# Two attention-and-mixer layers on one core: cutting the second layer's keys where the mixers finish, and more places for filler matmuls

## The chip, the cores and the metric

The kernel runs on one core of one Trainium2 chip. The metric is device time in microseconds (us) of one execution. All engines of the core work from instruction lists that are fixed at build time: TensorE (PE) multiplies matrices, ScalarE (ACT) does exponentials and GELUs, VectorE (DVE) and GpSimd (POOL) do element-wise work, and SyncE (SP) issues most transfers (DMAs).

## The reference

The input x is 2048 rows of 448 numbers. Two equal layers with shared weights follow each other; each is an attention part A and a mixer part B, both on a normalised x and both added back:

```
x = x + A(layernorm(x))      # 16 heads of 28: softmax(q k^T / sqrt(28)) v, then @ wo
x = x + B(layernorm(x))
# B(x): h  = gelu(layernorm(x) @ w1); its four column groups are shifted by +1, -1, +2, -2 rows
#       x1 = x + shifted(h) @ w2
#       return x1 + gelu(layernorm(x1) @ w3) @ w4
```

Because the mixer shifts rows by at most two, a tile of 128 rows can be mixed as soon as its two neighbours have left the attention. The second layer's attention needs the keys of all rows for each query row.

## The kernel before, in words

**Tiles and segments.** The 2048 rows are 16 tiles of 128. Keys, queries and values are made by projections from a transposed, normalised copy of x (xT), which is loaded from DRAM (xnd) into one of two buffers (XT, L654). The 16 heads are four groups g of four heads. CHUNKS (L493) cuts the queries into chunks of 4 tiles (the last one of the second layer into 2 and 2). ORDER (L494) lists, for each layer, which query chunk meets which range of key tiles: an entry (query chunk, first key tile, end key tile) becomes four segments, one for each g. In the second layer it begins

```
(0, 0, 4), (0, 4, 8), (1, 0, 8), (0, 8, 12), (1, 8, 12), (0, 12, 16), (1, 12, 16), (2, 0, 16), ...
```

so the first two query chunks take the keys in parts, as these become ready. Keys are projected in chunks of 4 tiles.

**The stream.** A block is one head, one key tile and 512 queries. All blocks of both layers stand in one list. They are grouped into 819 units of alternately 3 and 2 blocks. Unit by unit PE writes scores into banks 0 to 2 or 3 and 4 of PSUM (`score_ops`, L1125, recorded at L1138), ACT takes the exponential of the unit in one instruction (`t_exp`, L1213), and PE multiplies it with the values into bank 5 (`t_pv`, recorded with other plain matmuls at L697). The units alternate between the two sets of banks. The other projections, mixer products and statistics share the banks that `misc` (L678) gives: banks 6 and 7, and, before the stream holds them, also 5, 4 and 3.

**The running bound.** Instead of a row maximum, the exponent is shifted by a bound from the norms of queries and keys. `k_proj` (L960) projects the keys of a chunk for one g, squares them and reduces the squares to a maximum (kmaxc, L981); `t_bias` (L1086) turns the maxima of all chunks so far into the bound; `q_proj` (L986) adds it to the queries. If a later part of the keys brings a larger bound, `t_fct` (L1104) makes the difference (dbc, L1108) and a factor for what is accumulated, and `t_qp` (L1155) corrects the queries (L1160). So a part of the keys can only begin when all chunks that it reaches have their maxima, for all four g.

**The mixers.** When all four g of a query chunk have been normalised (`t_norm`, L1319: sums to DRAM and back, otn at L1357), `t_outproj` (L1393) makes the output projection (added to x_res at L1408), `t_mixA` (L1429) the first half of the mixer, and `t_mixB` (L1566) the second half. Since a tile needs its right neighbour, the second half runs in groups of tiles 0-2, 3-6, 7-10, 11-13 and 14-15 in the first layer (BGROUPS, L1419). GELUs stand on ACT between the exponentials, with a table load before and after. Then `t_ln1_l1` (L926) normalises a finished tile and stores it for the second layer.

**What sets the order.** A planner (`Sched`, L175) runs at build time. It holds a generator for each piece of work with a priority (smaller goes first), a cost for each instruction (`c_ps` for DVE reading PSUM, `c_act`, `c_mm`, fixed numbers for small operations), and writes each engine's list in the order of its own clock. MIXP (L442) gives the priorities of mixers, KVP (L446) those of key, value and query projections of a chunk: in the second layer 3 for chunk 0 and 1.5 for the others; the mixers of the first layer's last chunk have 1.6.

**Filler.** `keep_pe_busy` (L268) puts filler matmuls (L1643, four matmuls of 256 columns each) into gaps of PE's plan, when the share of work in the last WIN us is below TARGET. A filler writes only into bank 6 or 7 and only while nothing holds that bank.

**The beginning.** `t_ln1_first` (L877) normalises and transposes the first four tiles, projects g = 0 and lets the stream start; g = 1 to 3 follow. For g = 0 the squares are taken by ACT straight from PSUM (`square_first`, L954) and the query's own norm is added in PSUM; for the others POOL squares the copy in SBUF (`square`, L957) and DVE adds the norm (L1027).

Of the kernel before, what the change touches and what calls it, by code (L numbers as in the profile page):

```python
# [174 lines left out]
class Sched:  # L175
    LAT = 0.2
    EARLY = 0.25
    WIN = 3.42
    TARGET = 0.5

    def __init__(self, P):
        self.P = P
        self.cur = {e: 0.0 for e in ENGS}
        self.tasks = []
        self.seq = 0
        self.pe_mode = None
# [9 lines left out]
        self.recent = []  # L196

# [4 lines left out]
    def _advance(self, t):  # L202
        changed = False
        while True:
# [13 lines left out]
            elif c == "sig":  # L218
                self.events.add(spec[1])
                self.evt_t[spec[1]] = self.clock  # L220
            elif c == "rel":
                self.busy[spec[1]] = False
# [45 lines left out]
    def keep_pe_busy(self, until):  # L268
# [3 lines left out]
        while self.cur["pe"] + dur + 0.12 < until:  # L272
# [7 lines left out]
            for b in banks:  # L280
                if self.busy.get(b, False):
# [14 lines left out]
    def run(self):  # L296
        P = self.P
        while True:
# [121 lines left out]
            op = P.add(eng, fn, reads, writes, kw.get("deps", ()), dma, t_end)  # L420
            if start > self.clock:
# [20 lines left out]
def MIXP(L, ch):  # L442
    return {(0, 0): 3, (0, 1): 3, (0, 2): 1.6, (0, 3): 1.6, (1, 0): 3, (1, 1): 3, (1, 2): 2.5, (1, 3): 2, (1, 4): 1.6}[(L, ch)]


def KVP(L, c):  # L446
    return {(0, 1): 1.5, (0, 2): 1.6, (0, 3): 1.7, (1, 0): 3, (1, 1): 1.5, (1, 2): 1.5, (1, 3): 1.5}[(L, c)]
# [6 lines left out]
def build_kernel(nc, A_x, A_wqkv, A_wo, B_x, B_w1, B_w2, B_w3, B_w4, out, n_layers=2):  # L454
# [23 lines left out]
    def c_ps(n):  # L478
        return 0.07 + n * 0.00104
# [10 lines left out]
    def c_mm(n):  # L490
# [4 lines left out]
             1: [(0, 0, 4), (0, 4, 8), (1, 0, 8), (0, 8, 12), (1, 8, 12), (0, 12, 16), (1, 12, 16), (2, 0, 16), (3, 0, 16), (4, 0, 16)]}  # L495

    segs = []
    for L_ in range(2):
        for (ch_, a_, b_) in ORDER[L_]:
            for g_ in range(4):  # L500
                segs.append((L_, ch_, g_, (a_ // 4, b_ // 4), list(range(a_, b_)), a_ == 0, b_ == NT))
    first_e = {}
    for L_ in range(2):
        for (ch_, a_, b_) in ORDER[L_]:
            if a_ == 0:
                first_e[(L_, ch_)] = b_ // 4
# [75 lines left out]
    with st:  # L582
# [40 lines left out]
        kmaxc = sb("kmaxc", [128, 2, 4, NCH], FP32)  # L623
        k2 = sb("k2", [128, 2, 5, 4], FP32)
        bcb = sb("bcb", [128, 2, 5, 4], BF16)
        bc29 = sb("bc29", [128, 2, 5, 4], FP32)
        dbc = sb("dbc", [128, 2, 5, 4], FP32)
        db29 = sb("db29", [128, 2, 5, 4], FP32)
        fct = sb("fct", [128, 2, 5, 4], FP32)
# [48 lines left out]
        def misc(*reads):  # L678
            return ("acq", MISC if ("tail",) in SC.events else MISC[0:5], list(reads))
# [7 lines left out]
        def kslot(L, c):  # L687
            return c if L % 2 == 0 else (4, 5, 0, 1)[c]

        def vslot(L, t):  # L690
            return 4 * kslot(L, t // 4) + t % 4
# [60 lines left out]
        def t_setup():  # L752
# [39 lines left out]
            b = yield ("acq", MISC[0:5])  # L792
# [41 lines left out]
        def stats(src, t, rkeys):  # L834
            yield op("dve", 0.55, lambda e: e.bn_stats(out=st6[:, t, :], in_=src), reads=rkeys, writes=[("st6", t)])
            yield op("dve", 0.12, lambda e: e.bn_aggr(out=mv[:, t, :], in_=st6[:, t, :]), reads=[("st6", t)], writes=[("mv", t)])
# [103 lines left out]
        def load_xT(L, c, xt):  # L940
            for t in range(4 * c, 4 * c + 4):
                yield ("wait", ("xnd", L, t))
            yield dma("sp", lambda e: e.dma_start_transpose(out=xT[:, xt, :, :], in_=xnd[512 * c:512 * c + 512, :]),
                      reads=[("xnd", t) for t in range(4 * c, 4 * c + 4)], writes=[(("xT", xt), i) for i in range(4)], t=TRL_T)


        def proj(xt, g, wpad, wnm):
            b = yield misc(("xT", xt), (wnm,))
            for fc in FCS:
                yield op("pe", c_mm(512), mm4(ps[:, bi(b), :], wpad[:, fc, 128 * g:128 * g + 128], xT[:, xt, fc, :], fc == 0, fc == 3),  # L950
# [3 lines left out]
        def square_first(b, si):  # L954
            return op("act", c_act(512), lambda e: e.activation(out=sq[:, si, :], in_=ps[:, bi(b), :], func=ACT.Square), reads=[("ps", bi(b))], writes=[("sq", si)])

        def square(si, src, rk):  # L957
            return op("pool", 1.2, lambda e: e.tensor_tensor(out=sq[:, si, :], in0=src, in1=src, op=ALU.mult), reads=rk, writes=[("sq", si)])  # L958

        def k_proj(L, c, g, xt):  # L960
            b = yield from proj(xt, g, wk_pad, "wk_pad")
            c0 = kcol(L, 4 * c)
            dst = kT[:, g, c0:c0 + 512]
            dk = [("kT", g, vslot(L, 4 * c + i)) for i in range(4)]
            fast = L == 0 and c == 0 and g == 0
            if fast:
                s = yield ("acq", SQ)
                si = num(s)
                yield square_first(b, si)
            yield op("dve", c_ps(512), lambda e: e.tensor_scalar(out=dst, in0=ps[:, bi(b), :], scalar1=MK, scalar2=None, op0=ALU.add),  # L970
                     reads=[("ps", bi(b)), (("cols",), 2)], writes=dk, touch=[b],
                     alt=[alt("act", c_act(512), lambda e: e.activation(out=dst, in_=ps[:, bi(b), :], func=ACT.Identity, bias=MK))])
            yield ("rel", b)
            if not fast:
                s = yield ("acq", SQ, dk)
                si = num(s)
                yield square(si, dst, dk)
            b2 = yield misc(("sq", si))
            yield op("pe", c_mm(512), mm4(ps[:, bi(b2), :], astat[:, :], sq[:, si, :], True, True), reads=[("sq", si), ("astat",)], writes=[("ps", bi(b2))], touch=[b2], mode="col4")
            yield ("rel", s)  # L980
            yield op("dve", c_ps(512), lambda e: e.reduce_max(out=kmaxc[:, L, g, c:c + 1], in_=ps[:, bi(b2), :], axis=AX.X),  # L981
# [4 lines left out]
        def q_proj(L, qc, g, xt):  # L986
# [6 lines left out]
            p0 = first_e[(L, [ci for ci in range(len(CHUNKS[L])) if CHUNKS[L][ci][0] // 4 == qc][0])]  # L993
# [746 lines left out]
```

## Time and profile before

| | us |
|---|---|
| median of 3 runs | 1208.27 |
| lowest and highest run | 1207.6, 1210.52 |
| profiled execution, its own time | 1204.26 |
| span in its trace | 1202.5 |
| PE busy in the span | 1058.9 |
| ACT busy in the span | 1059.7 |
| DVE busy | 452.2 |
| POOL busy | 382.7 |

The trace comes from one profiled execution. Its own time is the span from the first to the last instruction and 1.76 us around it; it lies 4.01 us under the median of the plain runs. In a row of a timeline the first number is the start in us from the beginning of the span, the second the time taken (of a run of equal instructions from the start of the first to the end of the last), then engine, line, operation, what is written and read, and in brackets the idle time of that engine just before it with what ended it. A row of a group gives the count, the busy time in us and the mean of one instruction in ns.

### The profile page before, as it was taken

What the parts mean: (1) busy time and instruction counts of PE and PEld (TensorE: products, weight loads), DVE (VectorE), ACT (ScalarE), POOL (GpSimd) and SP (SyncE); (2) the same over time, 40 slices, a digit from 0 to 9 for tenths busy, and PEclk for the clock granted to TensorE, in tenths of its full rate; (3) what the DMA queues carried; (4) which work ended last, traced back from release to release, by engine and by line L of the source; (5) the groups of instructions that cost most, each with busy time, mean ns of one, the idle gap of its engine ahead of it and who ended that gap; (6) DMA issues with size and microseconds to landing.
All of it is one profiled execution on the core that took longest, in us unless ns stands there. A gap on an engine that the chain in (4) does not pass through costs nothing.

```text
span 1202.5 us, 34008 instructions
## 1 busy us (share of the span) xinstructions
PE 1058.9 (88%) x15542; PEld 417.7 (35%) x15542; DVE 452.2 (38%) x921; ACT 1059.7 (88%) x906; POOL 382.7 (32%) x396
## 2 busy tenths in 40 slices
PE   5998888889888899898988998988889898889888
PEld 2333333343323332223332433332323433334355
DVE  8464213331242235331643353423352433233243
ACT  3768999999989999989999958998989999899932
POOL 4931114403325054412343240202427501252201
PEclk9899999899979999998998999998999998899899
DMA  3384112002111032011231021324321110220000
GB/s 102 83 242 103 38 51 46 15 17 71 27 30 29 11 107 46 11 19 48 75 94 35 20 90 44 106 89 112 60 38 35 26 45 22 45 47 11 10 17 22
DMA packets 95784, 64.28 MB, mean 53 GB/s; under 512 B 64664, under 2 KB 84440, under 8 KB 95640
## 3 DMA queue, kind: packets, MB, share of 16 engines
q1 hardware_dynamic: 92376, 57.63, 19.2%
q0 software_dynamic: 2304, 3.67, 1.2%
q8 instruction: 122, 2.00, 0.7%
q10 hardware_dynamic: 960, 0.80, 0.2%
q14 instruction: 22, 0.18, 0.1%
HBM read 28.16 MB, written 16.76 MB: 37 GB/s over the span
## 4 chain that ended last, share of the span: by engine, by line
ACT 40%; PE 37%; DMA 8%; DVE 7%; POOL 5%; issue 1%; SPq 0%; ACTq 0%; POOLq 0%; DVEq 0%
ACT PT L1213 34%; PE ps L706 21%; PE ps L1138 9%; PE ps L697 6%; DMA rb<-rscr 4%; ACT h2T L1604 3%; POOL xn L850 2%; DMA xT<-xnd 1%; POOL otn L1357 1%; ACT hT L1488 1%; DMA rscr<-rT 1%; PE ps L1643 1%; DVE kmaxc L981 1%; DMA rT<-ub 1%; ACT L1604 1%
## 5 line engine op out<-in xcount | busy, mean ns | idle before, releaser
L1213 ACT ACTIVATE PT<-ps 128x1536 bf16<-128x1536 f32 (+1 forms) x819 | 939.3, 1307 | 59.2 <-PE ps L1138 56.6
L1138 PE MATMUL ps<-qT,kT 32*128 32x512 bf16 (+1 forms) x2304 | 326.5, 368 | 52.2 <-ACT PT L1213 43.6
L697 PE MATMUL ps<-PT,vaug 128*32 128x512 bf16 (+1 forms) x2304 | 254.1, 367 | 2.0 <-DVE ub L1335 2.0
L1138 PEld LDWEIGHTS ps<-qT,kT 32*128 32x128 bf16 x2304 | 80.3, 91 | 342.6 <-ACT PT L1213 271.7
L1643 PE MATMUL ps<-wq_pad,ident 128*32 128x256 bf16 x3836 | 182.4, 282 | 2.1 <-DVE x1b L1547 1.0
L706 PE MATMUL ps<-xT,w 128*32 128x512 bf16 (+1 forms) x2240 | 173.2, 367 | 6.9 <-issue 4.7
L706 PE MATMUL ps<-w,h2T 128*32 128x448 bf16 x1792 | 123.5, 382 | 20.8 <-ACT h2T L1604 20.8
L1357 POOL TENSOR_TENSOR otn<-ub,rb 128x512 bf16<-128x512 f32 (+1 forms) x32 | 38.6, 1205 | 320.6 <-DMA rb<-rscr 314.1
L1643 PEld LDWEIGHTS ps<-wq_pad,ident 128*32 128x32 bf16 x3836 | 108.9, 98 | 43.3 <-issue 23.8
L1594 DVE CAST h2T<-ps 128x512 bf16<-128x512 f32 (+2 forms) x126 | 73.9, 586 | 121.0 <-PE ps L706 112.6
L697 PEld LDWEIGHTS ps<-PT,vaug 128*32 128x32 bf16 x2304 | 69.8, 95 | 102.1 <-issue 85.4
L706 PEld LDWEIGHTS ps<-xT,w 128*32 128x32 bf16 x2240 | 59.0, 96 | 63.8 <-issue 38.1
L706 PEld LDWEIGHTS ps<-w,h2T 128*32 128x32 bf16 x1792 | 49.7, 102 | 68.6 <-issue 27.3
L850 POOL TENSOR_SCALAR xn<-x_res,mv,mst 128x448 bf16<-128x448 f32 x30 | 55.6, 1865 | 1.9 <-DVE mst L1451 1.9
L958 POOL TENSOR_TENSOR sq<-qT 128x512 bf16<-128x512 bf16 x31 | 32.1, 1040 | 73.0 <-DVE qT L1001 68.8
L850 POOL TENSOR_SCALAR xn<-x1b,mv,mst 128x448 bf16<-128x448 f32 x29 | 54.5, 1879 | 1.7 <-POOL mst L1553 0.2
L1333 DVE COPY ub<-ps 128x512 f32<-128x512 f32 (+1 forms) x36 | 22.7, 630 | 85.4 <-PE ps L697 85.2
L958 POOL TENSOR_TENSOR sq<-kT 128x512 bf16<-128x512 bf16 x31 | 32.2, 1041 | 66.6 <-DVE kT L970 63.5
L706 PE MATMUL ps<-w,hT 112*32 112x448 bf16 x512 | 40.9, 414 | 13.8 <-ACT hT L1488 13.5
L706 PE MATMUL ps<-xT,wq_pad 128*32 128x512 bf16 x512 | 44.8, 420 | 6.2 <-DMA xT<-xnd 5.5
L706 PE MATMUL ps<-wo_pad,otn 128*32 128x448 bf16 x512 | 42.0, 378 | 9.1 <-POOL otn L1357 6.1
L1604 ACT ACTIVATE h2T<-h2T 128x7168 bf16<-128x7168 bf16 (+2 forms) x9 | 45.1, 5015 | 3.9 <-DVE h2T L1594 3.8
(134 smaller groups left out, 869.4 us busy)
## 6 DMA issues: line engine op xcount, KB each, us to landing
uscr<-ub SPq DMA_DIRECT2D x28, 256.0 KB
ub<-uscr SPq DMA_DIRECT2D x28, 256.0 KB
rb<-rscr SPq DMA_DIRECT2D x28, 256.0 KB
xnd<-xn SPq DMA_DIRECT2D x28, 128.0 KB, 2.0
x_res<-in_A_x_dram POOLq DMA_DIRECT2D x16, 224.0 KB, 3.5
xd<-x_res SPq DMA_DIRECT2D x16, 224.0 KB, 2.1
x_res<-xd SPq DMA_DIRECT2D x16, 224.0 KB
out_dram<-obf SPq DMA_DIRECT2D x16, 112.0 KB
```

The source lines that it names most:

```text
L697: return lambda e: e.matmul(out=out, lhsT=lhsT, rhs=rhs, start=start, stop=stop, **kw)
L706: r.append(e.matmul(out=out[c:c + w, :], lhsT=lhsT[:, c:c + w], rhs=rhs, start=start, stop=stop, tile_position=(0, c)))
L850: yield op(eng, dur, lambda e: e.tensor_scalar(out=xn[:, k, 0:D], in0=src, scalar1=scalar1, scalar2=scalar2, op0=ALU.subtract, op1=ALU.mul ...
L958: return op("pool", 1.2, lambda e: e.tensor_tensor(out=sq[:, si, :], in0=src, in1=src, op=ALU.mult), reads=rk, writes=[("sq", si)])
L981: yield op("dve", c_ps(512), lambda e: e.reduce_max(out=kmaxc[:, L, g, c:c + 1], in_=ps[:, bi(b2), :], axis=AX.X), reads=[("ps", bi(b2))], ...
L1138: yield op("pe", max(0.055, 0.22 / nc_ * NW / 512.0), lambda e, i=i, kc=kc, j=j, g=g, a=a, NW=NW, bank=bank: e.matmul(out=ps[:, bank, i * ...
L1213: yield op("act", 0.07 + n * 0.427, lambda e, bk=bk, s0=s0, n=n: e.activation(out=PT[:, s0:s0 + n, :], in_=ps[:, bk[0]:bk[0] + n, :], func ...
L1333: yield op("dve", c_ps(NW), lambda e: e.tensor_copy(out=u, in_=ps[:, 5, 0:NW]), reads=[("ps", 5)], writes=[uk])
L1357: yield op("pool", 0.2 + NW * 0.0021, lambda e: e.tensor_tensor(out=otn[:, g, 0:NW], in0=u, in1=rb[:, 0:NW], op=ALU.mult), reads=[uk, ("rb ...
L1594: ev = op("dve", c_ps(NW), lambda e, fch=fch, b=b: e.tensor_copy(out=h2T[:, fch, 0:NW], in_=ps[:, bi(b), 0:NW]), reads=[("ps", bi(b))], wr ...
L1604: yield op("act", c_act(14 * NW), lambda e: e.activation(out=h2T[:, :, 0:NW], in_=h2T[:, :, 0:NW], func=ACT.Gelu_apprx_tanh), reads=allk, ...
L1643: return [e.matmul(out=ps[32 * c:32 * c + 32, bi(b), 0:256], lhsT=ident[:, 32 * c:32 * c + 32], rhs=wq_pad[:, 0, 0:256], start=True, stop= ...
```

## The change

1. The second layer's keys are projected in chunks of 3, 4, 4, 3 and 2 tiles (a new table KC) in place of four chunks of 4. Bounds, maxima and transposed loads follow the new chunks (there are five for the second layer), with narrower projections for 3 and 2 tiles; the keys and values of the second layer lie in other places of their buffers.
2. The second layer's first two query chunks take the keys in parts of 7, 4 and 5 tiles, one after the other.
3. Priorities: the mixers of the first layer's last chunk go from 1.6 to 1.4, the second layer's key chunks 1 and 2 from 1.5 to 2.5; chunk 4 gets 1.5.
4. In the first layer's first chunk all four g take the short way: squares by ACT, the query's norm added in PSUM.
5. `misc` gives banks 6, 7 and 5 in place of 6, 7, 5, 4 and 3 (also in the set-up). `q_proj` waits for its bound before it takes a bank, except for the very first.
6. Filler: WIN 2.3 for 3.42, TARGET 0.52 for 0.5, and seven banks (6, 7, 0 to 4) for two. A bank may be filled while it is "dead", that is from the planned end of its last reader (the exponential, or the release of the bank) until PE writes it again.
7. The planner's costs for several DVE and POOL instructions are other numbers, mostly larger for DVE; the instructions are the same.

The core of the diff:

```diff
-    WIN = 3.42
-    TARGET = 0.5
+    WIN = 2.3
+    TARGET = 0.52
...
-                if self.busy.get(b, False):
+                if b not in self.dead:
...
-(0, 3): 1.6, (1, 0): 3, ...
+(0, 3): 1.4, (1, 0): 3, ...
...
-    return {..., (1, 0): 3, (1, 1): 1.5, (1, 2): 1.5, (1, 3): 1.5}[(L, c)]
+    return {..., (1, 0): 3, (1, 1): 2.5, (1, 2): 2.5, (1, 3): 1.5, (1, 4): 1.5}[(L, c)]
...
-        return 0.07 + n * 0.00104
+        return 0.13 + n * 0.00108
...
-             1: [(0, 0, 4), (0, 4, 8), (1, 0, 8), (0, 8, 12), (1, 8, 12), (0, 12, 16), (1, 12, 16), (2, 0, 16), (3, 0, 16), (4, 0, 16)]}
+             1: [(0, 0, 7), (1, 0, 7), (0, 7, 11), (1, 7, 11), (0, 11, 16), (1, 11, 16), (2, 0, 16), (3, 0, 16), (4, 0, 16)]}
+    KC = {0: [(0, 4), (4, 4), (8, 4), (12, 4)], 1: [(0, 3), (3, 4), (7, 4), (11, 3), (14, 2)]}
+
+    def kc_of(L, t):
+        return [c for c, (a, n) in enumerate(KC[L]) if a <= t < a + n][0]
+
+    def ext_of(L, t):
+        return 0 if t == 0 else kc_of(L, t - 1) + 1
...
-            return ("acq", MISC if ("tail",) in SC.events else MISC[0:5], list(reads))
+            return ("acq", MISC if ("tail",) in SC.events else MISC[0:3], list(reads))
...
-            return 4 * kslot(L, t // 4) + t % 4
+            return t if L == 0 else (t + 17 if t < 7 else t - 7)
...
-            fast = L == 0 and c == 0 and g == 0
+            fast = L == 0 and c == 0
...
+            if idx > 0 or g > 0:
+                yield ("wait", ("bc", L, p0, g))
             b = yield from proj(xt, g, wq_pad, "wq_pad")
...
-            if idx == 0 and g == 0:
+            if idx == 0:
...
+                for b in bk:
+                    yield ("dead", "b%d" % b)
                 yield ("sig", ("ex", u))
...
-        SC.fill = (0.12, filler, ["b6", "b7"], lambda b: ("ps", bi(b)), [("ident",), ("wq_pad",)])
+        SC.fill = (0.12, filler, ["b6", "b7", "b0", "b1", "b2", "b3", "b4"], lambda b: ("ps", bi(b)), [("ident",), ("wq_pad",)])
```

More of the change, by code (lines that the diff above doesn't have):

```diff
@@ L196, in __init__ @@
         self.recent = []
+        self.dead = set("b%d" % i for i in range(8))
+        self.bank_of = {("ps", i): "b%d" % i for i in range(8)}
     def spawn(self, gen, prio=5):
@@ L960, in k_proj, with square @@
+        def square(si, src, rk, NW=512):
+            return op("pool", 0.15 + NW * 0.0018, lambda e: e.tensor_tensor(out=sq[:, si, 0:NW], in0=src, in1=src, op=ALU.mult), reads=rk, writes=[("sq", si)])
         def k_proj(L, c, g, xt):
[L961 to L964, printed above, removed]
-            fast = L == 0 and c == 0 and g == 0
+            t0, n = KC[L][c]
+            NW = 128 * n
+            b = yield from proj(xt, g, wk_pad, "wk_pad", NW)
+            c0 = kcol(L, t0)
+            dst = kT[:, g, c0:c0 + NW]
+            dk = [("kT", g, vslot(L, t0 + i)) for i in range(n)]
+            fast = L == 0 and c == 0
@@ L1032, in v_proj @@
             yield ("wait", ("vinit",))
-            for i in range(4):
-                t = 4 * c + i
+            t0, n = KC[L][c]
+            for i in range(n):
+                t = t0 + i
                 vs = vslot(L, t)
@@ L1047, in t_kv @@
         def t_kv(L, c):
-            for t in range(4 * c, 4 * c + 4):
+            t0, n = KC[L][c]
+            for t in range(t0, t0 + n):
                 yield ("wait", ("xnd", L, t))
@@ L1077, in t_q @@
             xt = num(x_)
-            yield from load_xT(L, qc, xt)
+            yield from load_xT(L, 4 * qc, 4, xt)
             yield ("sig", ("qloaded", L, qc))
```

104 lines of the change are left out of this document (54 added, 50 removed).

## The prediction

> **What bounds the kernel now.** I read the page first, then ACT's timeline around each gap, then what PE and DVE do there.
>
> ```profile
> PE 1058.9 (88%) x15542; PEld 417.7 (35%) x15542; DVE 452.2 (38%) x921; ACT 1059.7 (88%) x906; POOL 382.7 (32%) x396
> ACT  3768999999989999989999958998989999899932
> L958 POOL TENSOR_TENSOR sq<-kT 128x512 bf16<-128x512 bf16 x31 | 32.2, 1041 | 66.6 <-DVE kT L970 63.5 <-PE ps L706 3.1
> L1213 ACT ACTIVATE PT<-ps 128x1536 bf16<-128x1536 f32 (+1 forms) x819 | 939.3, 1307 | 59.2 <-PE ps L1138 56.6
> L1643 PE MATMUL ps<-wq_pad,ident 128*32 128x256 bf16 x3836 | 182.4, 282 | 2.1 <-DVE x1b L1547 1.0
> ```
>
> The slices of ACT are the reading: 9 nearly everywhere, low in the first three, 5 once in the middle, low in the last two. In between the stream of exponentials is the bound: 819 units in 939.3 us, 1.147 us each. PE's 88% holds 182.4 us of filler, so it has room. A change gains only where ACT has no unit to work on. The start:
>
> ```profile
> 23.59 1.45 ACT L1213 ACTIVATE PT<-ps 128x1536 bf16<-128x1536 f32 x1 [1.22 <-PE ps L1138]
> 35.97 3.28 ACT L1213 ACTIVATE PT<-ps 128x1024 bf16<-128x1024 f32 x3 [10.92 <-PE ps L1138]
> 42.95 21.92 ACT L1213 ACTIVATE PT<-ps 128x1536 bf16<-128x1536 f32 x19 [0.90 <-PE ps L1138]
> 73.25 0.21 ACT L1113 ACTIVATE fct<-dbc 128x4 f32<-128x4 f32 x1 [8.37 <-DVE dbc L1108]
> 107.95 0.20 ACT L1113 ACTIVATE fct<-dbc 128x4 f32<-128x4 f32 x1 [3.63 <-DVE dbc L1108]
> 109.06 11.40 ACT L1213 ACTIVATE PT<-ps 128x1024 bf16<-128x1024 f32 x10 [0.90 <-PE ps L1138]
> ```
>
> Unit 0 runs, then 10.92 us of nothing: unit 1 needs banks 3 and 4, which the projections of the first chunk still hold. Then two waits for a bound (dbc): keys of chunk 1, and of chunks 2 and 3. From 109 on ACT is full until the layers meet:
>
> ```profile
> 694.26 13.94 ACT L1213 ACTIVATE PT<-ps 128x1536 bf16<-128x1536 f32 x12 [1.26 <-PE ps L1138]
> 722.52 0.20 ACT L1113 ACTIVATE fct<-dbc 128x4 f32<-128x4 f32 x1 [14.32 <-DVE dbc L1108]
> 723.63 4.86 ACT L1213 ACTIVATE PT<-ps 128x1536 bf16<-128x1536 f32 x4 [0.91 <-PE ps L1138]
> 729.48 1.45 ACT L1213 ACTIVATE PT<-ps 128x1536 bf16<-128x1536 f32 x1 [0.98 <-PE ps L1138]
> 738.56 3.19 ACT L1604 ACTIVATE h2T<-h2T 128x3584 bf16<-128x3584 bf16 x1
> 741.77 1.28 ACT L1213 ACT_TABLE_LOAD   x1
> 743.07 41.00 ACT L1213 ACTIVATE PT<-ps 128x1536 bf16<-128x1536 f32 x36
> ```
>
> At 708.20 the exponentials end and resume at 723.63: 15.43 us, plus 0.98 at 729.48. This is key chunk 2 (tiles 8 to 11), of which tile 11 comes with the first layer's last but one mixer group.
>
> **The change, part by part.**
>
> *Parts of 7, 4 and 5 tiles.* At 708.20 the stream has used what it could reach: two query chunks against 8 key tiles, 2 x 8 x 16 = 256 blocks. With chunks of 3, 4, 4 it reaches 11 tiles, 352 blocks, without the last two mixer groups. The 96 more blocks are 38.4 units, at 1.147 us 44.0 us; the GELU of the last group falls into them, 1.28 + 3.19 + 1.28 = 5.8 us. So ACT has work until 708.2 + 44.0 + 5.8 = 758.0, and 15.4 + 1.0 = 16.4 us of waiting go.
>
> What is late next is the part (11 to 16). It needs the bound over chunks 3 and 4, so the very last mixer group. In the trace that bound is there at 783.36:
>
> ```profile
> 588.39 1.28 POOL L1357 TENSOR_TENSOR otn<-ub,rb 128x512 bf16<-128x512 f32 x1 [1.35 <-DMA rb<-rscr]
> 598.34 1.14 DVE L1408 TENSOR_TENSOR x_res<-x_res,ps 128x448 f32<-128x448 f32 x2
> 612.95 0.60 DVE L1408 TENSOR_TENSOR x_res<-x_res,ps 128x448 f32<-128x448 f32 x1
> 722.34 0.15 DVE L1108 TENSOR_TENSOR dbc<-bcb 128x4 f32<-128x4 bf16 x1
> 751.04 0.62 DVE L1616 TENSOR_TENSOR x_res<-x_res,ps 128x448 f32<-128x448 f32 x1 [2.63 <-PE ps L706]
> 766.05 0.75 DVE L970 TENSOR_SCALAR kT<-ps,cols 128x512 bf16<-128x512 f32 x1 [3.12 <-PE ps L706]
> 783.36 0.15 DVE L1108 TENSOR_TENSOR dbc<-bcb 128x4 f32<-128x4 bf16 x1
> ```
>
> Unchanged it would leave a wait of 783.4 - 758.0 = 25.4 us, more than is removed. Three things move it forward. First, from 708.2 to 722.3 PE works on key chunk 2 and holds up the third product of the last group; in the changed kernel those keys are made long before: 14 us less, or, since exponentials now run there and take PE's time, about 10. Second, the last chunk's output projection: its input is there at 589.7, its last sum at 613.6, 24 us for four tiles, because key chunk 1 and query chunk 1 go first (1.5 against 1.6). With 1.4 against 2.5 it is the other way round; the two rows show two tiles added within 1.14 us, so most of the 24 us is queueing. I take 8 us. Third, from the last tile (751.7) to the bound (783.4) are 31.7 us, of which 17.3 are projections of four tiles in no hurry; two tiles are half as wide. I take 5. That is 783.4 - 10 - 8 - 5 = 760, a wait of 2 us (bounds: 0, and 25 if nothing moves). Net gain 16.4 - 2 = 14.
>
> PE's share bears this out. From 575 to 708:
>
> ```profile
> L1138 PE MATMUL ps<-qT,kT 32*128 32x512 bf16 x255 | 40.6, 393 | 5.7 <-ACT PT L1213 5.2
> L697 PE MATMUL ps<-PT,vaug 128*32 128x512 bf16 x260 | 32.4, 386 | 0.0
> L706 PE MATMUL ps<-xT,wk_pad 128*32 128x512 bf16 x64 | 5.5, 384 | 0.0
> L706 PE MATMUL ps<-wv,xT 128*32 128x448 bf16 x64 | 5.5, 354 | 0.0
> ```
>
> Scores and values take 73.0 of 133 us, 55%, so the rest of the work runs at 45% of PE. A key chunk costs 5.5 + 5.5 us of PE and its norms; chunk 1 leaves this stretch for one before it and chunk 2 enters it, so its load stays. The stretch before gets three tiles' worth, about 9 us. Filler covers it (182.4 us in all, 0.15 per us of span, so 23 us in 155); without that cover it would cost up to 9 us. I put 1.
>
> *The start.* With banks 3 and 4 never lent out, unit 1 follows unit 0, and 10.92 + 0.90 us go there, if groups 1 to 3 keep up with two or three banks. Six squares move from POOL (1.04 us each) to ACT, which is idle there, at 0.6 each: 3.6 us that push the stream back. DVE loses three adds.
>
> ```profile
> L955 ACT ACTIVATE sq<-ps 128x512 bf16<-128x512 f32 x2 | 1.2, 597 | 7.0 <-PE ps L706 7.0
> 36.38 1.88 POOL L850 TENSOR_SCALAR xn<-h2T,mv,rstd 128x448 bf16<-128x448 bf16 x1
> 57.36 0.81 PE L706 MATMUL ps<-xT,wk_pad 128*32 128x512 bf16 x8
> L1138 PE MATMUL ps<-qT,kT 32*128 32x512 bf16 x85 | 13.1, 384 | 1.5 <-DVE qT L1160 1.3 <-ACT PT L1213 0.2
> L697 PE MATMUL ps<-PT,vaug 128*32 128x512 bf16 x88 | 10.9, 383 | 0.0
> ```
>
> The first part's 25.6 units would end near 23.6 + 25.6 x 1.147 + 3.6 = 56.6 instead of 64.9. But then the stream waits for chunk 1, so the gain is only what chunk 1 and then 2 and 3 gain. Their projections begin at 57.36, and from there to 109 scores and values take 13.1 + 10.9 us of PE for 33 units, 0.73 each. Seven of these units (57.4 to 64.9) would be done before, which frees 5 us of a full PE. The normalising of chunk 1 begins on POOL at 36.38; with the squares gone from ahead of it I take 2 us. Gain 7 us; bounds 0 (the chain from load to keys is as long as now) and 11.8 (the whole hole).
>
> *Filler.* The trace shows what a gap on PE costs:
>
> ```profile
> 547.08 3.77 PE L1643 MATMUL ps<-wq_pad,ident 128*32 128x256 bf16 x124
> 554.24 5.42 PE L706 MATMUL ps<-w,h2T 128*32 128x448 bf16 x56 [3.39 <-ACT h2T L1604]
> 689.38 4.51 PE L706 MATMUL ps<-w,h2T 128*32 128x448 bf16 x56 [2.12 <-ACT h2T L1604]
> 741.81 2.45 PE L706 MATMUL ps<-w,h2T 128*32 128x448 bf16 x48 [2.05 <-ACT h2T L1604]
> 560.09 20.73 ACT L1213 ACTIVATE PT<-ps 128x1536 bf16<-128x1536 f32 x18 [2.23 <-PE ps L1138]
> 1016.12 17.27 ACT L1213 ACTIVATE PT<-ps 128x1536 bf16<-128x1536 f32 x15 [2.51 <-PE ps L1138]
> ```
>
> During a GELU the fillers run off as one burst (31 in 3.77 us), PE idles 3.39 us, and 56 products then take 5.42 us where 48 took 2.45 after 2.05 us: half speed, and the scores come 2.23 us late. So it is also at 694.26 (1.26) and 1016.12 (2.51). With WIN 2.3 filler begins sooner after the last work and with 0.52 there is 4% more: about 0.4 us more burst, so 3.0 us of idling. After 2.12 us PE was at 4.51 already, so I expect most of it to stay. Banks 0 to 4 help little at a GELU, since they hold the scores that wait for ACT; they are dead at the start and where a bound is missing. I put a gain of 2 us (bounds: 4 lost by filler in front of real work, 8 gained).
> [...]
>
> *Nothing for the rest.* The larger costs in the planner change the order alone, the new places of keys and values move no more data, and the tail after the last exponential has the same instructions. Reordering can shift waits of 1 to 3 us either way; I put 0, with 4 to both sides.
>
> Sum: -14 + 1 - 7 - 2 = -22 us. The profiled execution, 1204.3 (span 1202.5), would become 1182, and the median, 4.0 above it, 1186.
>
> **The rivals.**
>
> *The start gains nothing* (0.17): chunk 1's keys hang on loads and POOL, and the hole moves from 25-36 to just before 73. For: chunk 1's xT and not the stream starts PE's work at 57.36. Against: the squares ahead of it on POOL. Time 1193.
>
> *Filler clears the half-speed spells* (0.12): if 3.0 us is short enough, the waits of 2.23, 1.26, 2.51 and their like go, 8 us in place of 2, and with 2 us more of small waits that go with them the time is 1178. For: the spells follow gaps of PE. Against: the half speed after 2.12 us.
> [...]
>
> *The new wait is half as long as the old one* (0.09): the bound at 769 rather than 760, a wait of 11. Time 1195; with little gain at the start up to 1202.
>
> *Slower, by the two xT buffers* (0.09): key chunks 1 and 2, now at 2.5, keep a buffer from load to last projection; the mixers of the last chunk need one three times. If a mixer waits for a chunk that nobody hurries, the bound of 783.36 comes later, not sooner. The price is one for one: beyond 758 + 2 + 22 = 782 the whole gain is gone; at 792 the time is 1218. For: nothing in the planner passes a waiting mixer's priority to the holder of its buffer. Against: PE has 45% of its time for such work.
>
> *No change* (0.05): the rest of the order turns out that much worse; 1208.
>
> **How the numbers follow.** The forecast's own case has 0.48, 1179 to 1193. Faster by over 0.3% (3.6 us, about what a measurement of this kernel can tell from no change) are the forecast and the first three rivals, 0.86; the same 0.05; slower 0.09. The range goes from 1174 (start 11, filler 8, no new wait: 4 + 6 + 2 under the forecast) to 1203 (the third rival with a poor start) and leaves out the two last cases and the edge of the second.
>
> **What would show it.** Right: ACT's 10.92 us near 25 gone and the stream into the second part before 70; no wait for dbc near 700, one of 0 to 5 us before the third part, near 745; L1408 of the last chunk close behind its otn; 900 to 1200 filler groups of four instead of 959 (3836 / 4), with PE still at half speed after GELUs. Wrong: a wait for dbc of over 15 us before the third part, a first wait for dbc still ending at 73, or new waits of ACT for scores of together over 8 us.

## The result, and the profile after

| | before | after |
|---|---|---|
| median, us | 1207.93 (4 runs) | 1161.47 (4 runs) |
| lowest, highest | 1202.34, 1210.52 | 1160.91, 1162.26 |
| profiled execution, own time | 1204.26 | 1161.40 |
| its span | 1202.5 | 1159.7 |
| mean granted clock of PE in it (1 is full speed) | 0.956 | 0.978 |

The ratio is 0.9622, with a 95% interval of 0.9588 to 0.9656: 46 us less. The forecast was 22 us less (1186), and the time lies below its range.

Line numbers have moved: the exponential is L1233 (was L1213), the scores L1158 (L1138), values L711 (L697), other products L720 (L706), filler L1665 (L1643), the first GELU of a mixer (hT) L1510 (L1488), the second (h2T) L1626 (L1604), dbc L1128 (L1108), fct L1133 (L1113), otn L1379 (L1357). In the experiments they shift again by a few lines. From the page of the changed kernel (busy time, ACT's slices, two groups):

```profile
PE 1040.8 (90%) x15790; PEld 420.4 (36%) x15793; DVE 446.1 (38%) x909; ACT 1057.8 (91%) x910; POOL 376.9 (32%) x394
...
ACT  5868999999999998899999999999799999999932
...
L1233 ACT ACTIVATE PT<-ps 128x1536 bf16<-128x1536 f32 (+1 forms) x819 | 934.8, 1325 | 36.9 <-PE ps L1158 36.1
...
L1665 PE MATMUL ps<-wq_pad,ident 128*32 128x256 bf16 x4016 | 185.2, 279 | 2.4 <-POOL wq_pad L802 1.1
```

The 5 in the middle of ACT's row is gone. The same 819 exponentials take the same time (934.8 us, before 939.3), so what was gained is idle time of ACT. The table of waits names it (total us, times, longest), before and after:

```profile
ACT PT L1213 <- PE ps L1138: 56.6, 51, 10.9
ACT fct L1113 <- DVE dbc L1108: 26.3, 3, 14.3
```

```profile
ACT PT L1233 <- PE ps L1158: 36.1, 33, 5.7
...
PE ps L720 <- POOL otn L1379: 12.9, 5, 5.6
...
ACT fct L1133 <- DVE dbc L1128: 8.7, 3, 4.7
```

20.5 us less waiting for scores and 17.6 less for bounds (dbc) make 38 of the 42.8 us of span; the row of otn comes up again at e11. The filler is 4016 / 4 = 1004 groups, near the 959 of before.

Since ACT carries the stream, the gain can be placed by asking when unit n starts in either trace (the last two columns are differences to before; "keys alone" is the experiment e8 below):

| unit | before, us | after, us | after | keys alone |
|---|---|---|---|---|
| 25 (second part of keys) | 74.34 | 62.61 | -11.7 | -1.4 |
| 55 | 113.54 | 108.08 | -5.5 | -1.4 |
| 420 | 587.54 | 575.93 | -11.6 | -4.5 |
| 500 | 694.26 | 679.21 | -15.1 | -1.3 |
| 560 (third part is running) | 786.21 | 756.25 | -30.0 | -17.1 |
| 818 (last) | 1144.58 | 1104.54 | -40.0 | -20.5 |

The steps show the meeting of the layers (15 us between units 500 and 560), as forecast; at the start, 11.7 us of which 6 are given back; and 10 us each in the long stretches before (units 55 to 500) and behind (560 to 818), where the forecast had only the 2 us of the filler.

The start, in ACT's timeline of the changed kernel (start, time taken, in brackets the idle time before and its end):

```profile
39.47 17.38 ACT L1233 ACTIVATE PT<-ps 128x1536 bf16<-128x1536 f32 x15
61.52 0.20 ACT L1133 ACTIVATE fct<-dbc 128x4 f32<-128x4 f32 x1 [4.66 <-DVE dbc L1128]
62.61 11.50 ACT L1233 ACTIVATE PT<-ps 128x1024 bf16<-128x1024 f32 x10 [0.89 <-PE ps L1158]
79.42 1.02 ACT L1233 ACTIVATE PT<-ps 128x1024 bf16<-128x1024 f32 x1 [5.31 <-PE ps L1158]
...
102.49 0.20 ACT L1133 ACTIVATE fct<-dbc 128x4 f32<-128x4 f32 x1 [2.71 <-DVE dbc L1128]
```

The hole of 10.92 us is gone and the second part starts at 62.6. But at 79.42 there is a wait that before did not have. PE's timeline shows its origin:

```profile
77.80 1.05 PE L720 MATMUL ps<-xT,wk_pad 128*32 128x512 bf16 x8 [5.18 <-DMA xT<-xnd]
```

PE's list has a projection of the next chunk ahead of the scores, and stands 5.18 us for its transposed load. The stream came 11.7 us earlier, but this load was issued only 8.6 us earlier than before (at 73.42 against 82.06).

The meeting of the layers, ACT's timeline again:

```profile
706.32 36.27 ACT L1233 ACTIVATE PT<-ps 128x1536 bf16<-128x1536 f32 x32
743.96 0.21 ACT L1133 ACTIVATE fct<-dbc 128x4 f32<-128x4 f32 x1 [1.37 <-DVE dbc L1128]
745.06 20.45 ACT L1233 ACTIVATE PT<-ps 128x1536 bf16<-128x1536 f32 x18 [0.90 <-PE ps L1158]
```

No wait for a bound near 700; ahead of the third part one of 1.37 + 0.90 = 2.27 us (forecast: 2). DVE's timeline gives the first and last sum of the last chunk's output projection, POOL's the otn they follow:

```profile
577.98 0.62 DVE L1430 TENSOR_TENSOR x_res<-x_res,ps 128x448 f32<-128x448 f32 x1 [0.96 <-PE ps L720]
...
583.76 0.60 DVE L1430 TENSOR_TENSOR x_res<-x_res,ps 128x448 f32<-128x448 f32 x1
```

```profile
576.16 1.27 POOL L1379 TENSOR_TENSOR otn<-ub,rb 128x512 bf16<-128x512 f32 x1 [0.42 <-DMA rb<-rscr]
```

From the end of otn (577.4) to the last sum (584.4) are 7 us, where before had 24.

### The profile page after: what moved, and what is told of

The parts are those of the page before. It is cut to its first block, busy times and chain, and to the rows that moved or that the text cites. A ratio compares the mean times of both kernels' runs of the same rounds, so it can differ in the third digit from the quotient of the medians.

```text
span 1159.7 us, 34479 instructions
## 1 busy us (share of the span) xinstructions
PE 1040.8 (90%) x15790; PEld 420.4 (36%) x15793; DVE 446.1 (38%) x909; ACT 1057.8 (91%) x910; POOL 376.9 (32%) x394
## 4 chain that ended last, share of the span: by engine, by line
ACT 60%; PE 26%; DMA 5%; DVE 4%; POOL 3%; issue 1%; SPq 1%; POOLq 0%; DVEq 0%
ACT PT L1233 52%; PE ps L720 14%; PE ps L1158 6%; PE ps L711 5%; ACT h2T L1626 3%; DMA rb<-rscr 2%; ACT L1233 1%; ACT hT L1510 1%; ACT L1510 1%; DMA xT<-xnd 1%; DMA xnd<-xn 1%; ACT L1626 1%; POOL otn L1379 1%; POOL xn L864 1%; DVE xn L864 1%
## 5 line engine op out<-in xcount | busy, mean ns | idle before, releaser
L1233 ACT ACTIVATE PT<-ps 128x1536 bf16<-128x1536 f32 (+1 forms) x819 | 934.8, 1325 | 36.9 <-PE ps L1158 36.1
L1158 PE MATMUL ps<-qT,kT 32*128 32x512 bf16 (+1 forms) x2304 | 323.2, 365 | 46.5 <-ACT PT L1233 33.5
L711 PE MATMUL ps<-PT,vaug 128*32 128x512 bf16 (+1 forms) x2304 | 258.5, 365 | 0.5 <-ACT PT L1233 0.5
L1158 PEld LDWEIGHTS ps<-qT,kT 32*128 32x128 bf16 x2304 | 80.3, 91 | 338.5 <-ACT PT L1233 295.3
L1665 PE MATMUL ps<-wq_pad,ident 128*32 128x256 bf16 x4016 | 185.2, 279 | 2.4 <-POOL wq_pad L802 1.1
L720 PE MATMUL ps<-xT,w 128*32 128x512 bf16 (+1 forms) x2240 | 172.1, 367 | 4.5 <-issue 3.5
L1379 POOL TENSOR_TENSOR otn<-ub,rb 128x512 bf16<-128x512 f32 (+1 forms) x32 | 38.5, 1202 | 289.9 <-DMA rb<-rscr 279.8
L720 PE MATMUL ps<-w,h2T 128*32 128x448 bf16 x1792 | 117.3, 360 | 14.3 <-ACT h2T L1626 14.3
L1665 PEld LDWEIGHTS ps<-wq_pad,ident 128*32 128x32 bf16 x4016 | 113.9, 98 | 37.1 <-issue 17.7
L711 PEld LDWEIGHTS ps<-PT,vaug 128*32 128x32 bf16 x2304 | 71.1, 95 | 100.8 <-issue 87.0
L720 PEld LDWEIGHTS ps<-xT,w 128*32 128x32 bf16 x2240 | 59.0, 96 | 60.9 <-issue 33.6
L720 PEld LDWEIGHTS ps<-w,h2T 128*32 128x32 bf16 x1792 | 47.8, 97 | 55.9 <-issue 18.8
L972 POOL TENSOR_TENSOR sq<-kT 128x512 bf16<-128x512 bf16 (+2 forms) x32 | 29.8, 933 | 97.9 <-DVE kT L986 97.7
L1626 ACT ACTIVATE h2T<-h2T 128x7168 bf16<-128x7168 bf16 (+2 forms) x9 | 45.1, 5016 | 15.6 <-DVE h2T L1616 15.6
L720 PE MATMUL ps<-xT,wk_pad 128*32 128x512 bf16 (+2 forms) x576 | 48.7, 371 | 6.1 <-DMA xT<-xnd 5.2
L720 PE MATMUL ps<-wo_pad,otn 128*32 128x448 bf16 x512 | 40.7, 379 | 13.0 <-POOL otn L1379 12.9
L1357 DVE SCALAR_TENSOR_TENSOR ub<-ub,fct,ps 128x512 f32<-128x512 f32 x24 | 17.9, 747 | 73.5 <-PE ps L711 71.5
L1430 DVE TENSOR_TENSOR x_res<-x_res,ps 128x448 f32<-128x448 f32 x32 | 19.9, 620 | 66.7 <-PE ps L720 66.5
L972 POOL TENSOR_TENSOR sq<-qT 128x512 bf16<-128x512 bf16 x28 | 29.0, 1039 | 50.6 <-DVE qT L1019 47.6
```

What stands on the lines that cost most here:

```text
L711: return lambda e: e.matmul(out=out, lhsT=lhsT, rhs=rhs, start=start, stop=stop, **kw)
L720: r.append(e.matmul(out=out[c:c + w, :], lhsT=lhsT[:, c:c + w], rhs=rhs, start=start, stop=stop, tile_position=(0, c)))
L972: return op("pool", 0.15 + NW * 0.0018, lambda e: e.tensor_tensor(out=sq[:, si, 0:NW], in0=src, in1=src, op=ALU.mult), reads=rk, writes=[( ...
L1158: yield op("pe", max(0.055, 0.22 / nc_ * NW / 512.0), lambda e, i=i, kc=kc, j=j, g=g, a=a, NW=NW, bank=bank: e.matmul(out=ps[:, bank, i * ...
L1233: yield op("act", 0.07 + n * 0.427, lambda e, bk=bk, s0=s0, n=n: e.activation(out=PT[:, s0:s0 + n, :], in_=ps[:, bk[0]:bk[0] + n, :], func ...
L1379: yield op("pool", 0.2 + NW * 0.0021, lambda e: e.tensor_tensor(out=otn[:, g, 0:NW], in0=u, in1=rb[:, 0:NW], op=ALU.mult), reads=[uk, ("rb ...
```

## The experiments

My first theory after the result: keys and start do as forecast, and the 24 us too much come from the filler. Rivals: the planner's new costs change the order for the better all along; or nothing in particular does, and one order of the lists differs from another by that much. Every run below is timed beside the kernel before on the same chip (medians of that: 1199.29 to 1202.35 us), so a ratio of 0.99 is 12 us. The changed kernel itself, run again as a control (c1), gave 0.9649 (0.9600 to 0.9698), 1161.1 us.

> The changed kernel itself, as the mark for the runs beside it on this chip. Ratio to the kernel before as it was, 0.959 to 0.966.

**One part taken out of the changed kernel.**

e1 has the old filler (rule, banks and constants):

```diff
-    WIN = 2.3
-    TARGET = 0.52
+    WIN = 3.42
+    TARGET = 0.5
...
-                if b not in self.dead:
+                if self.busy.get(b, False):
...
-["b6", "b7", "b0", "b1", "b2", "b3", "b4"]
+["b6", "b7"]
```

> The changed kernel with the old filler rules alone (WIN 3.42, TARGET 0.5, banks 6 and 7 only, and only while nothing holds them). Theory 1: the part of the gain that was not forecast (about 21 us) comes from half-speed spells of PE after GELUs that the new bank rule avoids, because the old rule refused banks that a mixer product held without having written them. Then this run is 18 to 24 us slower than the changed kernel, about 1182, has about 16 to 20 half-speed spells instead of 9, and no filler in the gaps before L1510's followers. Theory 2: the truer DVE costs or the mere reordering made it; then 1162 to 1167 and 9 to 12 spells. Theory 3: the keys and the start are worth more than forecast; then also 1162 to 1167.

Measured 0.9704 (0.9648 to 0.9760), 1167.3 us, 6 us above the changed kernel, and the interval overlaps that of c1. So Theory 1 does not hold in its size. The granted clock of e1 is 0.969, against 0.982 in c1 and 0.956 before: in the order of the changed kernel the old filler leaves less half speed than it did before. And e1 starts unit 500 at 678.99 us, as early as the changed kernel (679.21): the 10 us gained between units 55 and 500 are not the filler's there.

e3 has the old keys (parts, chunks of 4, priorities):

```diff
-             1: [(0, 0, 7), (1, 0, 7), (0, 7, 11), (1, 7, 11), (0, 11, 16), ...
+             1: [(0, 0, 4), (0, 4, 8), (1, 0, 8), (0, 8, 12), (1, 8, 12), (0, 12, 16), ...
...
-1: [(0, 3), (3, 4), (7, 4), (11, 3), (14, 2)]}
+1: [(0, 4), (4, 4), (8, 4), (12, 4)]}
...
-(0, 3): 1.4, (1, 0): 3
+(0, 3): 1.6, (1, 0): 3
...
-(1, 1): 2.5, (1, 2): 2.5, (1, 3): 1.5, (1, 4): 1.5}
+(1, 1): 1.5, (1, 2): 1.5, (1, 3): 1.5}
```

> The changed kernel with the old key chunks, order, places and priorities of the second layer. Theory 1: the stream's lag on the kernel before grows by 15 to 18 us where the layers meet, so this run is 14 to 18 us slower, 1176 to 1180, with a wait for dbc of 14 to 16 us there. Theory 3: 25 to 35 us slower, 1187 to 1197.

Measured 0.9832 (0.9773 to 0.9892), 1183.26 us: 22 us worse than the changed kernel, between the two theories.

e4 has the old start:

```diff
-            fast = L == 0 and c == 0
+            fast = L == 0 and c == 0 and g == 0
...
-            if idx == 0:
+            if idx == 0 and g == 0:
...
-MISC[0:3]
+MISC[0:5]
```

> The changed kernel with the old start alone (squares of groups 1 to 3 on POOL, misc with banks 3 and 4, no wait for the bound ahead of the bank). Forecast's step: about 7 us slower; from the stream's lag after the start 5 us, so 1166 to 1168, with the hole of about 11 us back after unit 0. Rival: the chain of loads sets the start, and it is within 1 us of the changed kernel, 1161 to 1163.

Measured 0.9643 (0.9582 to 0.9704), 1160.3 us: no difference. ACT's timeline of e4:

```profile
32.85 27.23 ACT L1231 ACTIVATE PT<-ps 128x1024 bf16<-128x1024 f32 x24 [7.42 <-PE ps L1156]
66.41 0.20 ACT L1131 ACTIVATE fct<-dbc 128x4 f32<-128x4 f32 x1 [6.33 <-DVE dbc L1126]
...
105.06 0.21 ACT L1131 ACTIVATE fct<-dbc 128x4 f32<-128x4 f32 x1 [3.59 <-DVE dbc L1126]
```

The hole is back (7.42 us), yet the bound of the third part comes only 2.6 us later than in the changed kernel (105.06 against 102.49). So of the start's 7 us, 2.6 reach unit 55 by this trace, and not even these can be seen at the end. Nor are they clear of the spread between executions: in the trace of c1, which has the new start, unit 55 begins at 111.49 us, later than in e4 (110.65).

e5 has the old costs of the planner:

```diff
-        return 0.13 + n * 0.00108
+        return 0.07 + n * 0.00104
...
```

and so on for the small DVE operations and one of POOL.

> The changed kernel with the planner's old costs alone; the instructions are the same, only their order differs. Theory 1 (filler explains what was not forecast): within 4 us of the changed kernel. Theory 2 (truer DVE costs remove small waits of ACT for scores between units 140 and 420, where the run with the old filler rules still gained 10 us on the kernel before): 8 to 14 us slower than the changed kernel, with more such waits there.

Measured 0.9701 (0.9674 to 0.9729), 1169.1 us, 8 us above the control on the same chip, the lower end of Theory 2.

**One part alone in the kernel before.**

e2 is before with the whole new filler, the reverse of e1's diff and the record of dead banks. e7 takes the bank rule alone, with the old constants and banks 6 and 7:

```diff
+        self.dead = set("b%d" % i for i in range(8))
...
+                    self.dead.add(spec[1])
...
-                if self.busy.get(b, False):
+                if b not in self.dead:
```

> The kernel before with the new filler rules alone. Theory 1: 18 to 24 us faster than before, about 1187, with fewer than 12 half-speed spells instead of 20. Theories 2 and 3: 1203 to 1209.

> The kernel before with one thing changed in the filler: a bank may be filled while it is dead, not only while nobody holds it; banks 6 and 7 only, WIN and TARGET as before. If the held banks are what kept filler out of the gaps at the mixers' first GELU, this alone has the larger part of the 13 us that the new filler rules gave the kernel before (0.989), and those gaps of 2.8 us shrink to about 1.4; if window and target do it, it is within 3 us of the kernel before.

Measured: e2 0.9888 (0.9855 to 0.9921), 1188.26 us; e7 0.9899 (0.9875 to 0.9923), 1191.61 us. The rule alone gives 12 us, and the whole filler 13, less than the 18 to 24 of Theory 1; constants and more banks add nothing that can be told from none. Nor is it a matter of reordering: without the fillers, the instruction lists of all engines in e2 and e7 are those of before, instruction for instruction. What the rule does is seen at a mixer's first GELU. PE's timeline before, and in e7:

```profile
352.67 0.39 PE L1138 MATMUL ps<-qT,kT 32*128 32x512 bf16 x2 [0.20 <-ACT PT L1213]
355.89 3.18 PE L706 MATMUL ps<-w,hT 112*32 112x448 bf16 x32 [2.83 <-ACT hT L1488]
```

```profile
347.86 1.82 PE L1654 MATMUL ps<-wq_pad,ident 128*32 128x256 bf16 x60
350.76 1.70 PE L715 MATMUL ps<-w,hT 112*32 112x448 bf16 x32 [1.08 <-ACT hT L1499]
```

Before has no filler there: PE stands 2.83 us, and 32 products take 3.18 us. In e7 filler runs for 1.82 us, the idle is 1.08, and the same 32 products take 1.70. The granted clock (the 1.00 or 0.50 after POOL's column) in windows of the kernel before, around that place:

```profile
350.00:355.00 5.00, 2.86 (x30) 0.72 (x27) 1.10 (x2) 4.97 (x5) 0.00 (x0) 1.00 0.01 3
355.00:358.40 3.40, 2.51 (x28) 1.10 (x32) 0.73 (x2) 3.37 (x3) 0.00 (x0) 0.50 0.00 0
358.40:361.80 3.40, 3.40 (x35) 0.92 (x31) 2.10 (x5) 2.77 (x4) 1.73 (x4) 0.50 0.00 0
```

Behind this gap of 2.83 us the clock is 0.50 for 6.8 us (355.00 to 361.80). The waits tell how general this is. Before, then e7:

```profile
PE ps L706 <- ACT h2T L1604: 20.8, 8, 3.9
...
PE ps L706 <- ACT hT L1488: 13.5, 6, 2.9
```

```profile
ACT PT L1222 <- PE ps L1147: 44.1, 47, 10.7
...
PE ps L715 <- ACT h2T L1615: 20.8, 8, 3.9
...
PE ps L715 <- ACT hT L1499: 6.3, 5, 1.4
```

PE's waits for the second GELU are the same to the tenth; those for the first fall from 13.5 to 6.3 us, none longer than 1.4. ACT's wait for scores falls by 12.5 us (from the 56.6 shown above), as much as the span (by 11.6, to 1190.9 us). The clock records in the traces of both kernels of this case have 1.00 and 0.50 alone, so with a granted clock of 0.956 the kernel before spent 1202.5 x 0.044 x 2 = 106 us at half speed; the same sum gives 48 for e7, at 0.980.

e1 shows the same from the other side: with the old rule in the changed kernel the gap is empty again.

```profile
341.20 0.39 PE L711 MATMUL ps<-PT,vaug 128*32 128x512 bf16 x1
344.10 3.18 PE L720 MATMUL ps<-w,hT 112*32 112x448 bf16 x32 [2.51 <-ACT hT L1510]
```

Why the old rule kept filler out is read from the code: `keep_pe_busy` fills a gap only when PE's next product is recorded, and by then that product holds its bank. The mixer's products behind the GELU take banks 6 and 7 when they are planned, ahead of the end of the GELU, so "nothing holds the bank" is false for the whole gap. "Dead until written" is true for it.

e6 is before with the planner's new costs:

> The kernel before with the planner's new costs alone. Theory 1: within 4 us of the kernel before. Theory 2: 8 to 14 us faster than the kernel before, most of it between units 140 and 420.

Measured 0.9995 (0.9966 to 1.0023), 1200.67 us: nothing. Yet at unit 500 its stream is 15 us ahead of before, and at unit 520 it is 4.7 us behind. Of the 15 us some 7 are no lead: a GELU with its two table loads (in e6's trace 1.28 + 4.68 + 1.28 = 7.24 us), which before has done by then, still lies ahead. The other 8 go at the meeting of the layers, as ACT's timeline of e6 shows, and the same wait stands in e3, which also keeps the old keys:

```profile
723.56 0.20 ACT L1113 ACTIVATE fct<-dbc 128x4 f32<-128x4 f32 x1 [21.73 <-DVE dbc L1108]
```

```profile
706.22 0.20 ACT L1133 ACTIVATE fct<-dbc 128x4 f32<-128x4 f32 x1 [20.98 <-DVE dbc L1128]
```

Before waits 14.32 us there. In these two, with the old keys, a stream that arrives earlier only waits longer: what is gained ahead of the meeting is lost at it. That is not so for every gain. In e7, old keys too, the stream is 9.5 us ahead at unit 500 and still 9.4 behind the meeting, because the bound itself comes sooner:

```profile
713.07 0.21 ACT L1122 ACTIVATE fct<-dbc 128x4 f32<-128x4 f32 x1 [14.36 <-DVE dbc L1117]
```

That the filler also speeds PE up in the work that the bound waits for is the likely reason; no run shows it apart.

**Built up from the keys.** e8 has the keys alone (the changed kernel without new start, filler and costs), e9 keys and filler.

> The kernel before with the new key chunks, parts, places and priorities alone (start, filler and costs as before). The forecast's step: 14 us faster than before (0.988), with the wait at the meeting of the layers down from 14 us to 0 to 3. Theory A (the parts do not add up: key chunks also keep what other parts gain ahead of the meeting, and are worth 17 to 18 us only together with them): 11 to 16 us faster here. Theory B (the keys are worth 17 to 25 us by themselves): 0.979 to 0.986.

> The kernel before with the new keys and the new filler rules (start and costs as before). Theory A: at least the sum of both alone (keys 14, filler 13), 27 us or more faster, 0.973 to 0.978, and the 6 us to the changed kernel's 0.965 are start and costs. Rival: the two overlap and it is under 20 us faster.

Measured: e8 0.9871 (0.9831 to 0.9911), 1184.98 us, so 15.5 us for the keys; e9 0.9731 (0.9692 to 0.9770), 1168.69 us, so 16.8 more for the filler. The lists of e9 without the fillers are those of e8. ACT's timeline of e8 at the third part:

```profile
721.44 36.38 ACT L1231 ACTIVATE PT<-ps 128x1536 bf16<-128x1536 f32 x32 [0.98 <-PE ps L1156]
757.41 0.50 ACT L1131 ACTIVATE fct<-dbc 128x4 f32<-128x4 f32 x1
```

The third part begins at 757.4 with no wait at all; the forecast had work until 758.0 and the bound at 760.

**How much is one order worth?** LAT is the time that the planner allows for one engine to hear of another. A step of 0.01 us says nothing about the chip and deals another order.

```diff
-    LAT = 0.2
+    LAT = 0.21
```

e10 does this to the changed kernel, e13 to e9; e12 and e14 go the other way, to 0.19.

> The changed kernel with the planner's latency between engines at 0.21 in place of 0.2, a change with no meaning of its own: it shows what mere reordering does to the time. If it stays within 3 us of the changed kernel, the 6 us that the old costs lost are an effect of the costs; if it moves by 5 us or more, they may be mere reordering.

> The changed kernel with the planner's latency at 0.19, the other neutral nudge. If the changed kernel's 0.962 to 0.965 stands at the lucky end of what its orders give, this lies nearer to the first nudge's 0.976; if the first nudge was an unlucky one, within 0.004 of the changed kernel.

> Keys and filler alone (the run before gave 0.973) with the planner's latency at 0.21. If start and costs are worth 8 to 10 us of their own, all three orders of this kernel lie above the mean of the changed kernel's three; if what they add is reordering, the two sets overlap and their means are within 4 us.

> Keys and filler alone with the planner's latency at 0.19; the third order of this set, read as the second.

| order | changed kernel | keys and filler |
|---|---|---|
| LAT 0.20 | 0.9622, 0.9649 | 0.9731 |
| LAT 0.21 | 0.9764 (0.9711 to 0.9817) | 0.9718 (0.9657 to 0.9779) |
| LAT 0.19 | 0.9698 (0.9659 to 0.9738) | 0.9745 (0.9702 to 0.9788) |

The changed kernel's orders spread from 0.9622 to 0.9764, 17 us. Their mean is 0.970 (0.9636, the mean of its two measurements, with 0.9764 and 0.9698), that of keys and filler 0.973: 4 us for start and costs together, less than the spread. The changed kernel has the best of its three orders. So the 8 us of e5, and that e4 shows none, say little about a part. The filler's differences are of another kind: e1 has the lists of the changed kernel, as e2 and e7 have those of before and e9 those of e8, so they hold no reordering.

**The planner's times for transfers.** In the changed kernel PE waits 12.9 us for otn, and ACT then for PE. The worst place, in the timelines of PE and of ACT:

```profile
837.41 1.31 PE L720 MATMUL ps<-wo_pad,otn 128*32 128x448 bf16 x12 [5.58 <-POOL otn L1379]
```

```profile
839.31 1.02 ACT L1233 ACTIVATE PT<-ps 128x1024 bf16<-128x1024 f32 x1 [5.66 <-PE ps L1158]
```

otn waits for a transfer of 256 KB, to which the planner gives 2.8 us. The view of the tile rb (durations, first and last start):

```profile
L1375 SPq DMA_DIRECT2D rb<-rscr x32: 515/534/574, 124.9 to 1039.3; - x32
L1379 POOL TENSOR_TENSOR otn<-ub,rb x32: 727/1268/1277, 130.1 to 1042.6; 128x512 bf16<-128x512 f32 x28, 128x256 bf16<-128x256 f32 x4
```

The first one is issued at 124.9 and otn starts at 130.1, 5.2 us later. e11 gives the planner this time. The second edit is the transposed load, which in the same trace takes 5.5 us from issue to landing (the view of its DMAs); 6.5 was my choice, and the two were not run apart. e15 is e11 with LAT 0.21, and e16 is e11 with TARGET 0.8 in place of 0.52.

```diff
-writes=[("rb",)], t=2.8)
+writes=[("rb",)], t=5.2)
...
-TRL_T = 5.0
+TRL_T = 6.5
```

> The changed kernel with two planned DMA times nearer to the trace: the broadcast of the reciprocal sums 5.2 in place of 2.8, the transposed load 6.5 in place of 5.0. PE waits in its list for otn (12.9 us) and for the loaded xT (6.4 us), and half-speed spells follow. If a planner that knows the true times moves this work behind other work, the waits halve and the time falls by 5 to 10 us; if the chain behind becomes late instead, it stays within 3 us.

> The changed kernel with the two truer DMA times and the planner's latency at 0.21. If the 7 to 10 us that the truer times gained are an effect of shorter waits of PE for otn, they stay under the changed kernel with the same nudge (0.976) by 7 us or more, with at most 3 us of waits for otn; if they were reordering, this is at 0.965 to 0.98.

> The version with the two truer DMA times and TARGET 0.8. The bursts at the second GELU of a mixer last about half of it now, and half-speed spells follow some of them. If the spells still cost, more filler there gives 3 to 6 us over the version with truer DMA times (0.956 to 0.957), about 0.952; if more filler stands in the way of real work, it is 0.96 or more.

Measured: e11 0.9561 (0.9525 to 0.9597), 1147.41 us; e15 0.9573 (0.9535 to 0.9611), 1151.32 us; e16 0.9536 (0.9490 to 0.9583), 1145.07 us, the fastest of all and faster than both kernels of this case. Two orders agree, and their mean, 0.9567, lies 16 us under the 0.970 of the changed kernel's orders. The waits in e11:

```profile
ACT PT L1233 <- PE ps L1158: 17.2, 24, 4.9
...
PE ps L720 <- POOL otn L1379: 0.4, 1, 0.4
```

PE's wait for otn has gone from 12.9 to 0.4 us, and ACT's for scores from 36.1 to 17.2; in e15 they are 1.6 and 25.6.

e16 has 6636 / 4 = 1659 filler groups and a clock of 0.997 in place of 0.988, but its interval overlaps e11's, so no gain is shown: it seems that the half speed left by then hardly lies on the path.

## Why the prediction was right or wrong

**Parts of 7, 4 and 5 tiles: right.** Forecast 14 us, alone 15.5 (10.7 to 20.3). The wait of 16.4 us went, and the new one is 2.27 us in the changed kernel and none in e8. Of the three things said to move the last bound forward, the queueing of the output projection was put too low: 24 us became 7 in the changed kernel, 17 rather than 8 us gained; the other two were not measured apart, and the whole came out nearly as forecast. With the rest of the change the keys are worth more than alone (e3 loses 22 us), because the old keys' wait eats a lead that comes from the order, as e6 and e3 show. The price of 1 us for keys moved into a fuller stretch is not contradicted: keys alone reach unit 500 1.3 us ahead, though they lose 3.2 us of their lead between units 420 and 500. The rivals of a longer wait and of held xT buffers did not come about.

**The filler: this step failed.** It said "Banks 0 to 4 help little at a GELU" and that PE would stay at half speed after GELUs, 2 us in all with an upper bound of 8. The words about banks 0 to 4 and about the second GELU hold (20.8 us of waits before and in e7). What I overlooked is that the new rule also frees banks 6 and 7 at the *first* GELU, where the profile of before shows gaps without any filler; I quoted only gaps behind the second GELU, which had filler. Measured: 12 us by the rule alone, 13 with the whole filler, 17 on top of the keys, and 6 when it is taken out of the changed kernel, all with the lists of the other instructions unchanged. So the term of 2 us was 10 to 15 us too small when the filler is added to the kernel before or to the keys, about half of the 24 us that the forecast missed. The rival of cleared spells named the right effect with the wrong cause and at half the size.

The length of a gap did not settle where half speed followed: in the kernel before it followed one of 2.83 us (the rows at e7), and in the changed kernel one of 3.27 us was followed by a clock of 1.00 (the rows at the end of this document).

**The start: the size was wrong.** 7 us forecast, 2.6 at unit 55 by e4 against the changed kernel, not clear of the spread between executions, and none that can be measured at the end. The rival "the start gains nothing" has the result right, though not its reason: the second part came 11.7 us earlier, and the next load's wait (5.18 us) took half of that back.

**"Nothing for the rest", 4 us to both sides: too narrow, the second step that failed.** Sum by measured parts: keys 15.5 and filler 16.8 make 32.3; the changed kernel has 42 to 45 (0.9649 and 0.9622 of 1201). The remaining 10 to 13 us go with start and costs in this order, but over three orders only 4 us are left on average. Shown is that an order which differs by nothing of substance moves the time by up to 17 us between the ends; how the 10 to 13 us divide into costs, start and a lucky order stays open. The nearest thing to a cause is that a transfer is planned too short (2.8 us for rb, against the 5.2 read from the trace), which leaves an order with waits in chance places (up to 5.6 us in the changed kernel), as the gain of e11 and e15 suggests.

## What to carry to other kernels

When a filler rule changes, look for the gaps that have no filler now, and ask which condition kept it out; the gaps that are filled already are not where it will act. In a list that a planner writes, measure two or three neutral variants before crediting a part with less than their spread, and give the planner the transfer times of the trace first. A gain ahead of a place where the stream waits for something else counts only once that wait is gone, or if the same gain brings that something forward too.

## What the runs showed of the hardware that I had not expected

In these traces the length of a gap alone did not decide whether PE's clock was halved behind it. From PE's timeline of the changed kernel, two gaps at second GELUs, each behind a burst of filler:

```profile
391.96 3.90 PE L1665 MATMUL ps<-wq_pad,ident 128*32 128x256 bf16 x136
399.12 2.27 PE L720 MATMUL ps<-w,h2T 128*32 128x448 bf16 x44 [3.27 <-ACT h2T L1626]
...
543.57 4.52 PE L720 MATMUL ps<-w,h2T 128*32 128x448 bf16 x56 [3.07 <-ACT h2T L1626]
```

After 3.27 us of idling 44 products took 2.27 us; after 3.07 us 56 took 4.52. The granted clock around the two gaps (behind POOL's column, as above):

```profile
395.50:399.00 3.50, 0.35 (x16) 0.07 (x4) 0.00 (x0) 3.50 (x1) 0.10 (x1) 1.00 0.02 5
399.00:402.00 3.00, 2.81 (x54) 1.31 (x58) 0.00 (x0) 2.97 (x4) 0.00 (x0) 1.00 0.00 0
540.50:543.50 3.00, 0.00 (x0) 0.00 (x0) 0.00 (x0) 3.00 (x1) 0.00 (x0) 1.00 0.02 5
544.30:547.70 3.40, 3.40 (x44) 1.53 (x36) 0.00 (x0) 2.88 (x3) 0.00 (x0) 0.50 0.00 0
```

Behind the longer gap the clock stays at 1.00, behind the shorter one it is 0.50 for 3.4 us. In the rows of before, behind the gap of 2.83 us, it is 0.50 for 6.8 us; the longest spell of before, one at the start (34.1 to 44.3), lasts 10.2. What besides its length decides what follows a gap is not shown: no run here moved one gap alone.
